# Chunked attention and a gated feed-forward layer on one core: the third block's first product computed plainly, the sums of w_in formed a block later, more output buffers at two boundaries

## The chip, the cores and the metric

The kernel runs on one NeuronCore of a Trainium2 chip. Its engines work side by side and wait for each other through semaphores: TensorE (PE, matmuls; PEld is its weight load), VectorE (DVE), ScalarE (ACT), GpSimd (POOL) and SyncE (SP), which here issues all DMA transfers. The metric is device time in microseconds (us) of one execution; of several runs the median counts.

## The reference, cut to what matters

```python
# q, k, v: 8 batches x 8 heads x 576 tokens x 64, float32;  w_in: 512 x 2048,  w_out: 2048 x 512
# attention inside chunks of 64 tokens
scores = np.matmul(q_c, k_c.transpose(0, 1, 2, 4, 3)) / np.sqrt(64)
scores = scores - np.max(scores, axis=-1, keepdims=True)
attn = np.exp(scores)
attn = attn / (np.sum(attn, axis=-1, keepdims=True) + 1e-09)
x = np.matmul(attn, v_c)            # then heads side by side: 4608 tokens x 512
h = x @ w_in                        # first product, 4608 x 2048
g = h * (1.0 / (1.0 + np.exp(-1.702 * h)))
out = g @ w_out                     # second product, 4608 x 512
```

## The kernel before, in words

The 4608 tokens are 9 blocks of 512 (36 tiles of 128). For each block the first product gives 16 pieces of 128 hidden columns, numbered g = 16n + j for block n; piece g is gated (`g_h`, `g_l`) and goes into the second product, which adds over the 16 pieces into four PSUM banks `po0` to `po3`, one for each tile of the block. At a block's last piece the banks are copied to `ob` buffers (lines 1286 to 1293, ScalarE for tiles 0 and 2, VectorE for 1 and 3) and stored (line 1298). Every matrix is carried as a high and a low word, and a product is three matmuls (low times high, high times high, high times low).

There are three forms of the first product. Blocks 0 and 1 use the plain one (`h_pe`, lines 1245 to 1247): 12 matmuls of 512 columns for each piece. Block 2 (`PLAIN = 2`) uses seven products in place of eight on halves of its own columns (`plan_seven`, lines 693 to 785, matmuls at lines 715 to 717): four phases `ph0` to `ph3` for every two pieces, 7 products of 6 matmuls, each of 256 columns, whose results VectorE and ScalarE add up (`drain_0` to `drain_3`, line 719). Blocks 3 to 8 are taken in pairs, two blocks side by side (`plan_two`, lines 787 to 900, matmuls at 810 to 812): seven products P1 to P7 of 512 columns for every two pieces of both blocks.

The seven products need sums and differences of w_in's parts and of x's parts. `plan_prep` (lines 584 to 649) forms those of w_in while block `PLAIN - 1` runs: GpSimd adds (`whole`, `sums`), ScalarE rounds (`hi`, line 608), VectorE takes the rest (`lo`, line 612), and SP writes the result to the DRAM tensor `seven` (lines 620, 623, 628), from which `plan_seven` (line 702) and `plan_two` (lines 801 and 803) load it. `plan_x` (lines 520 to 582) forms those of x. They stand in the first halves of the tiles `w0` to `w15`, which held w_in until then.

Attention is computed for pairs of tiles (`plan_pair(u)`, u = 4, 6, ... 34). For u from 6 on, 32 or 64 small transfers bring q and k (`load_qk`, lines 953 and 964) into the one buffer `raw`; VectorE transposes them (`tq0`, `tq1`, line 1007), TensorE multiplies (`s`, line 1023), VectorE takes the maximum and subtracts it (`mx`, `m`), ScalarE the exponential, VectorE the sum (`z`), GpSimd divides (line 1053), VectorE transposes again (`et`, line 1072), TensorE multiplies by v (line 1097, together with the next pair's `s`).

The order on each engine is set by the class `Plan`: each step has an engine, a cost, a rank, the events it needs and the buffers it takes and gives, and a list scheduler takes at each moment the ready step of lowest rank. `transfers` in that class is its model of the DMA queue. The order at the start is written out (`ORDER`). Each engine then executes its own list strictly in order. Two buffers `hp` (PSUM) take the first product and the result of attention; a piece's buffer is free when its `g_l` has been formed (line 1272 for plain pieces). The pool `two` holds two `ob` buffers, and the store of one must have landed before it is written again.

Of the kernel before, what the change touches and what calls it, by code (L numbers as in the profile page):

```python
# [9 lines left out]
F32 = mybir.dt.float32  # L10
# [37 lines left out]
class Plan:  # L48
# [8 lines left out]
    ISSUE, LANES, LANDING = 0.48, 8, 2.1  # L57
    TABLE_LOAD = 1.3

    def __init__(self, buffers):  # L60
        self.free = dict(buffers)
        self.steps = []
        self.landed = [0.0] * self.LANES
        self.first = {}


    def add(self, engine, cost, rank, fn, need=(), make=None, take=(), give=(), table=None, port=False):
        self.steps.append((engine, cost, rank, fn, tuple(need), make, tuple(take), tuple(give), table, port or engine == POOL))
# [4 lines left out]
    def transfers(self, now, count, each):  # L73

        for _ in range(count):
            start = max(now, self.landed[-self.LANES])
            now = start + self.ISSUE
            self.landed.append(max(start + self.LANDING, self.landed[-1] + each))
        return now, self.landed[-1]

    def emit(self):
# [18 lines left out]
        while left:  # L100
            for e, heap in ready.items():
                while heap and busy[e] <= now + 1e-9:
# [13 lines left out]
                    _, cost, _, fn, _, make, take, give, tab, port = self.steps[pick]  # L116
# [17 lines left out]
                    post(done, 0, give)  # L134
# [27 lines left out]
def tile_chunk_attention_ffn(  # L162
# [14 lines left out]
    P = 128  # L177
# [14 lines left out]
    RANKS = (-10.5, 9.0, 14.0, 21.0, 26.5, 28.5, 35.0, 39.0, 45.5, 49.5, 61.0, 72.0, 76.5, 85.5, 94.0, 101.5)  # L192
    K_ACT = (1, 2, 3, 4)
    LEAD = 27
    PREP = -3
    SUMS = 3
    ON_POOL = (0,)
    RING_2 = (7, 8, 0, 1, 5, 6)
# [15 lines left out]
    buffers.update({f"half{j}": 0 for j in RING_2})  # L214
# [13 lines left out]
    X_2 = (2, 3, 4)  # L228
    X_SLOT = (9, 10, 11, 12, 6, 2, 3, 7, 15, 5, 13, 14, 4, 8)
# [7 lines left out]

    def run_of(n):

        return (n - PLAIN + 1) // 2  # L240
# [8 lines left out]
    def plan_w(j):  # L249
# [48 lines left out]
        plan.add(DMA, (2, 1.56), rank - 5.5, load, need=need, make=e("raw"), take=[f"w{j}"])  # L298
# [49 lines left out]
    def plan_first(u):  # L348
# [109 lines left out]
        plan.add(DMA, (1, 1.2), u - 103, lambda: load(0), make=ev("q"), take=[slot(0)])  # L458
        plan.add(DMA, (1, 1.2), u - 102.9, lambda: load(1), make=ev("k"))
        plan.add(DMA, (1, 0.9), u - 101.5, load_v, make=ev("v"), take=[slot(1)])  # L460
# [32 lines left out]
    def x_2(i, hl):  # L493

        if i < 4:
            return held["x", i // 2][:, hl, i % 2]
        return wt[X_2[hl]][:, 0, i % 2] if i < 6 else wt[X_2[2]][:, 0, hl]

# [3 lines left out]
    def x_tile(k):  # L502
        held["x", k] = const.tile([P, 2, 2, 512], F32R, tag=f"xe{k}", name=f"xe{k}")

    def staging(u):

        r, i = (0, (u - 8) // 2) if u < 12 else divmod((u - 12) // 2, 4)
        if u < 12:
            return ("sA", "sB")[i]
        return (("sA", "xe2a", "xe2b", "xe3a") if r == 0 else ("sA", "xe3b", "tmp", "tmp"))[i]  # L510
# [9 lines left out]
    def plan_x(r, h, ua, uc, rank):  # L520

        st = {}
        where_t = "xe3b" if r == 1 else "tmp"
        T_ENGINE, T_COST, engine = (POOL, 1.05, nc.gpsimd) if r in ON_POOL else (DVE, 0.69, nc.vector)

        def raw(i, k=1):
# [3 lines left out]
            return d[:, 512 * at : 512 * (at + k)]  # L530
# [6 lines left out]
        def conv(i, k, hl):  # L537
            if r:
                return x_two(i, hl)[:, :, 256 * h : 256 * h + 256]
            if i == 6:  # L540
                return x_2(6, hl)
            t = held["x", i // 2][:, hl] if i < 4 else wt[X_2[hl]][:, 0]
            return t.rearrange("p i f -> p (i f)")

        form = lambda a: a.rearrange("p (c t) -> p c t", c=2) if r else a

        def hi(i, k):
            nc.scalar.activation(conv(i, k, 0), form(raw(i, k)), AF.Copy)

        def lo(i, k):  # L550
            nc.vector.tensor_tensor(conv(i, k, 1), form(raw(i, k)), conv(i, k, 0).bitcast(F32), op=ALU.subtract)

        e = lambda a: f"{a}x_{r}_{h}"
# [6 lines left out]
        for i in (0, 1, 5, 4, 2, 3, 6) if r else (0, 2, 4, 6):  # L560
            k = 1 if r or i == 6 else 2
            need = src[i] + (src[i + 1] if k == 2 else [])
            for hl in range(2):
                j = X_SLOT[2 * i + hl]
                if r == 0:
                    more_need = [f"po_{(X_2[hl] if i < 6 else X_2[2]) // 2}"] if i > 3 else [f"xal_{i // 2}"]
                elif r == 1:
                    g0 = NF * (PLAIN + 1) - 2
                    more_need = [f"po_{j // 2}" if j > 8 else f"ph{(1, 2, 3)[(j in (4, 7, 8)) + (j in (4, 8))]}_{g0}"]
                else:  # L570
                    more_need = [f"{PRODUCT_OF[i]}_{r - 2}_{NF // 2 - 1}"]
# [843 lines left out]
```

## Time and profile before

| | |
|---|---|
| runs | 845.22, 845.10, 842.77 us (median 845.1) |
| profiled execution | 844.18 us, span 842.4 us from first to last instruction |
| TensorE busy | 818.4 us, 97% |
| VectorE, ScalarE, GpSimd busy | 549.1 (65%), 378.4 (45%), 86.7 (10%) |
| mean granted TensorE clock | 0.993 |
| DMA | 128.96 MB, one queue of transfers (q1), 56.5% of 16 engines' span |

The page of the profile gives busy time by engine, the span in 40 slices, the chain of work that ended last, and groups of instructions by line. Where it isn't enough the trace answers by view: waits (who waited for whom), timelines of one engine in a stretch, and busy time with granted clock in a stretch. A clock of 1.00 is 2.4 GHz, 0.50 is 1.2 GHz. Matmuls are pipelined, so their pace is read from the distance of two starts and not from the duration of one.

### The profile page before, as it was taken

The page shows a single profiled execution, that of the slowest core. Times are in us where ns is not written, and L with a number is a line of the kernel's source. Part 1 is how long each engine was busy: PE and PEld are TensorE (multiplying, and loading weights), DVE is VectorE, ACT ScalarE, POOL GpSimd, SP SyncE. Part 2 cuts the span into 40 slices and gives each one's busy share as a digit, 9 for nine tenths or more (in the row PEclk, how much of TensorE's full clock was granted, in tenths as well). Part 3 has the DMA queues.
Part 4 walks back from the last instruction along what each step waited for, and adds up shares of the span by engine and source line. Part 5 has one row for each costly group of instructions (what it writes and reads, how often), then busy time and mean ns, then how long its engine had stood idle before and what let it go on. Part 6 is the DMA issues. An engine that isn't in the chain of part 4 may idle for free.

```text
span 842.4 us, 15212 instructions
## 1 busy us (share of the span) xinstructions
PE 818.4 (97%) x5894; PEld 680.0 (81%) x5894; DVE 549.1 (65%) x781; ACT 378.4 (45%) x557; POOL 86.7 (10%) x78
## 2 busy tenths in 40 slices
PE   7999998999979999999999999999999999999998
PEld 6878886877878888778888888888888888888786
DVE  5769967566867888874776995393778453443422
ACT  5989825345344436342534433342555323223322
POOL 1000163563200000000000100000001000000000
PEclk9999999999989999999999999999999999999999
DMA  9997856775488776575466336466541054444101
GB/s 227 313 309 239 251 130 163 208 202 134 129 244 218 212 209 141 169 175 147 125 179 176 62 79 173 126 152 155 145 128 49 1 165 121 118 122 126 50 1 51
DMA packets 238248, 128.96 MB, mean 153 GB/s; under 512 B 186464, under 2 KB 208992, under 8 KB 238176
## 3 DMA queue, kind: packets, MB, share of 16 engines
q1 hardware_dynamic: 238176, 127.98, 56.5%
q8 instruction: 47, 0.77, 0.4%
q14 instruction: 25, 0.20, 0.1%
HBM read 103.81 MB, written 24.12 MB: 152 GB/s over the span
## 4 chain that ended last, share of the span: by engine, by line
PE 81%; SPq 9%; DMA 4%; DVE 3%; issue 1%; ACT 1%; POOL 0%; DVEq 0%; ACTq 0%; POOLq 0%
PE po L1282 14%; PE po L1283 13%; PE po L1284 13%; PE hp L810 9%; PE hp L811 9%; PE hp L812 9%; SPq L964 3%; SPq L338 2%; PE hp L1245 2%; PE hp L1246 2%; PE hp L1247 2%; DMA w<-seven 2%; PE s L1023 2%; PE x L1097 1%; SPq L258 1%
## 5 line engine op out<-in xcount | busy, mean ns | idle before, releaser
L1282 PE MATMUL po<-w,g_l 128*128 128x512 f32 x576 | 228.1, 396 | 6.7 <-ACT ob L1291 4.8
L1283 PE MATMUL po<-w,g_h 128*128 128x512 f32 x576 | 225.0, 391 | 0.0
L1284 PE MATMUL po<-w,g_h 128*128 128x512 f32 x576 | 224.8, 390 | 0.0
L1282 PEld LDWEIGHTS po<-w,g_l 128*128 128x128 f32 x576 | 108.5, 188 | 32.3 <-ACT ob L1291 5.5
L1284 PEld LDWEIGHTS po<-w,g_h 128*128 128x128 f32 x576 | 108.4, 188 | 23.0
L1283 PEld LDWEIGHTS po<-w,g_h 128*128 128x128 f32 x576 | 108.5, 188 | 21.1
L848 ACT ACTIVATE g<-g 128x512 f32<-128x512 f32 x48 | 30.3, 632 | 143.3 <-DVE g L795 143.1
L1072 DVE STREAM_TRANSPOSE eT<-e 32x512 f32<-32x512 f32 x120 | 84.2, 701 | 5.4 <-POOL e L1053 3.5
L810 PE MATMUL hp<-w,w 128*128 128x512 f32 x224 | 87.4, 390 | 0.2
L811 PE MATMUL hp<-w,w 128*128 128x512 f32 x224 | 87.2, 389 | 0.0
L812 PE MATMUL hp<-w,w 128*128 128x512 f32 x224 | 87.2, 389 | 0.0
L1053 POOL TENSOR_TENSOR e<-e,r 128x1024 f32<-128x1024 f32 x16 | 32.2, 2012 | 502.1 <-DVE r L1050 397.6
L857 DVE TENSOR_TENSOR g_l<-g,g_h 128x512 fp32r<-128x512 f32 x48 | 35.2, 737 | 44.5 <-ACT g_h L853 44.2
L853 ACT ACTIVATE g_h<-g 128x512 fp32r<-128x512 f32 x48 | 30.3, 631 | 73.7 <-PE po L1284 71.4
L1007 DVE STREAM_TRANSPOSE qkT<-raw 128x1024 f32<-128x1024 f32 x30 | 37.2, 1241 | 27.8 <-DMA raw<-in_k_dram 15.7
L1245 PE MATMUL hp<-x_l,w 128*128 128x512 f32 x120 | 47.8, 398 | 5.8 <-DVE g_l L1272 5.8
L810 PEld LDWEIGHTS hp<-w,w 128*128 128x128 f32 x224 | 42.0, 188 | 9.9 <-DVE f L795 0.5
L812 PEld LDWEIGHTS hp<-w,w 128*128 128x128 f32 x224 | 42.0, 188 | 8.8
L811 PEld LDWEIGHTS hp<-w,w 128*128 128x128 f32 x224 | 42.0, 188 | 8.6
L1247 PE MATMUL hp<-x_h,w 128*128 128x512 f32 x120 | 47.4, 395 | 0.0
L1246 PE MATMUL hp<-x_h,w 128*128 128x512 f32 x120 | 47.4, 395 | 0.0
L795 DVE TENSOR_TENSOR d<-hp,d 128x512 f32<-128x512 f32 x48 | 32.9, 684 | 19.0 <-PE hp L812 18.7
(142 smaller groups left out, 1335.5 us busy)
## 6 DMA issues: line engine op xcount, KB each, us to landing
w<-seven SPq DMA_DIRECT2D x120, 256.0 KB, 2.9
pieces<-seven SPq DMA_DIRECT2D x56, 256.0 KB, 2.9
seven<-w SPq DMA_DIRECT2D x24, 512.0 KB, 3.7
w<-seven SPq DMA_DIRECT2D x24, 512.0 KB, 4.6
raw<-in_moe_w_in_dram SPq DMA_DIRECT2D x16, 512.0 KB, 7.5
raw<-in_moe_w_out_dram SPq DMA_DIRECT2D x16, 512.0 KB, 7.8
out_dram<-ob SPq DMA_DIRECT2D x32, 256.0 KB, 2.3
raw<-in_q_dram SPq DMA_DIRECT2D x208, 32.0 KB, 2.4
```

The lines of the kernel that those rows point to most:

```text
L810: nc.tensor.matmul(hp, w[:, 0, c], xl[:, c], start=c == 0, stop=False)
L811: nc.tensor.matmul(hp, w[:, 0, c], xh[:, c], start=False, stop=False)
L812: nc.tensor.matmul(hp, w[:, 1, c], xh[:, c], start=False, stop=c == 1)
L857: nc.vector.tensor_tensor(gl, words(h, late), gh.bitcast(F32), op=ALU.subtract)
L1007: nc.vector.transpose(st["tr"][:, i].rearrange("p n (t j) -> p (n t) j", j=32), st["raw"][:, i].rearrange("p n t j -> p (n t) j"),)
L1072: nc.vector.transpose(st["et"][po : po + 32, :, 32 * a : 32 * a + 32], st["e"][pi : pi + 32, :, 32 * b : 32 * b + 32],)
L1245: nc.tensor.matmul(hp, wh, xl, start=cc == 0, stop=False)
L1246: nc.tensor.matmul(hp, wh, xh, start=False, stop=False)
L1247: nc.tensor.matmul(hp, wl, xh, start=False, stop=cc == NCC - 1)
L1282: nc.tensor.matmul(po, gl[:, c], w[:, 0, :], start=first, stop=False)
L1283: nc.tensor.matmul(po, gh[:, c], w[:, 0, :], start=False, stop=False)
L1284: nc.tensor.matmul(po, gh[:, c], w[:, 1, :], start=False, stop=last)
```

## The change: what it does

`PLAIN` goes from 2 to 3: block 2 gets the plain first product, and `plan_seven` with its loads, drains and buffers is gone, as is the form of `plan_x` that served it. The pairs of blocks are the same three as before (3 and 4, 5 and 6, 7 and 8). Since `plan_prep` runs in block `PLAIN - 1`, the sums of w_in are formed in block 2 and not in block 1. The differences of x for the first pair of blocks (r = 0) are formed by GpSimd where VectorE formed them, and go to other slots (`X_SLOT`).

At the end of blocks 0 and 1 the third and fourth output tile go to buffers of their own (`sA`, `sB`, `xe3b`) in place of the two `ob`; later blocks keep the two.

Of the planner the model of the DMA queue changes (one queue with a bound on the pieces in flight; in both kernels SP issues every transfer, by `nc.sync`), and with it ranks: those of the attention pairs (`RANKS`), of stores (`STORE`, 22 before), of the late gates (`GLATE`, 1.5 before), and single steps moved by `NUDGE`. The written-out `ORDER` of the start is the same.

```diff
+    ISSUE, LANES, LANDING = 0.48, 8, 1.8
+    PIECES = 3072
...
             start = max(now, self.landed[-self.LANES])
+            while True:
+                flight = [(t, n) for t, n in self.flight if t > start]
+                if sum(n for _, n in flight) + pieces <= self.PIECES:
+                    break
+                start = flight[0][0]
             now = start + self.ISSUE
-            self.landed.append(max(start + self.LANDING, self.landed[-1] + each))
+            self.landed.append(max(start + self.LANDING, self.landed[-1]) + each)
+            self.flight = flight + [(self.landed[-1], pieces)]
...
-    RANKS = (-10.5, 9.0, 14.0, 21.0, 26.5, 28.5, 35.0, 39.0, 45.5, 49.5, 61.0, 72.0, 76.5, 85.5, 94.0, 101.5)
+    RANKS = (-2.0, 9.0, 14.0, 20.5, 23.5, 32.5, 33.0, 40.5, 45.0, 55.5, 63.5, 74.5, 74.5, 82.5, 93.5, 100.0)
...
-    ON_POOL = (0,)
+    GLATE = 29.5
+    XLATE = -1.0
+    STORE = 4
...
+    ON_POOL = (0, 3)
...
-    PLAIN = 2
-    TWOS = (NB - PLAIN - 1) // 2
-    START = [NF * (PLAIN + 1) + 30 * s for s in range(TWOS)]
+    PLAIN = 3
+    TWOS = (NB - PLAIN) // 2
+    START = [NF * PLAIN + 30 * s for s in range(TWOS)]
...
-    X_SLOT = (9, 10, 11, 12, 6, 2, 3, 7, 15, 5, 13, 14, 4, 8)
+    X_SLOT = (2, 3, 4, 5, 10, 11, 12, 13, 8, 9, 6, 7, 14, 15)
...
-    def plan_seven(n, p):
...
-        ob_tag = lambda t: ("ob", "ob", "raw", "tr")[t] if n == NB - 1 else "ob"
+        ob_tag = lambda t: {0: ("ob", "ob", "sA", "sB"), 1: ("ob", "ob", "sB", "xe3b"), NB - 1: ("ob", "ob", "raw", "tr")}.get(n, ("ob",) * 4)[t]
...
-            ob = (two if ob_tag(t) == "ob" else const).tile([P, DM], F32, tag=ob_tag(t), name=f"ob_{n}_{t}")
+            if ob_tag(t) in ("sA", "sB", "xe3b"):
+                ob = stage_tile(ob_tag(t), f"ob_{n}_{t}")[:, :DM]
+            else:
+                ob = (two if ob_tag(t) == "ob" else const).tile([P, DM], F32, tag=ob_tag(t), name=f"ob_{n}_{t}")
...
-            if n == PLAIN and j % 2 == 0:
-                plan_seven(n, j // 2)
-            elif n > PLAIN and (n - PLAIN) % 2 and j % 2 == 0:
+            if (n - PLAIN) % 2 == 0 and j % 2 == 0:
                 plan_two((n - PLAIN) // 2, j // 2)
```

How the order moves is shown at three places. The first is VectorE at the end of block 0 and the start of block 1. In the names the first number is the piece, the pair of tiles or the block: `g_l_16` is the low word of piece 16, `qkT_10` the transpose for pair 10, `ob_0_3` tile 3 of block 0; the last number only tells buffers apart. Before:

```order
L1272 TENSOR_TENSOR g_l_15_1348<-hp_15_1287,g_h_15_1347 128x512
L1031 TENSOR_REDUCE m_8_1437<-s_8_1361 128x16
L1111 TENSOR_TENSOR x_l_1_86<-x_6_0_1394,x_h_1_85 128x2x4x64
L1111 TENSOR_TENSOR x_l_1_86<-x_6_1_1395,x_h_1_85 128x2x4x64
L1040 TENSOR_TENSOR e_8_1436<-s_8_1361,m_8_1437 128x1024
L1293 COPY ob_0_1_1482<-po_0_1_442 128x512
L1293 COPY ob_0_3_1495<-po_0_3_533 128x512
L1272 TENSOR_TENSOR g_l_16_1492<-hp_16_1462,g_h_16_1491 128x512
L1007 STREAM_TRANSPOSE qkT_10_1511<-raw_10_1339 128x1024
L1047 TENSOR_REDUCE z_8_1528<-e_8_1436 128x16
```

Now, at the same place:

```order
L919 TENSOR_REDUCE m_8_1436<-s_8_1358 128x16
L999 TENSOR_TENSOR x_l_1_86<-x_6_0_1391,x_h_1_85 128x2x4x64
L999 TENSOR_TENSOR x_l_1_86<-x_6_1_1392,x_h_1_85 128x2x4x64
L1182 COPY ob_0_3_1459<-po_0_3_533 128x512
L1182 COPY ob_0_1_1472<-po_0_1_436 128x512
L928 TENSOR_TENSOR e_8_1435<-s_8_1358,m_8_1436 128x1024
L1158 TENSOR_TENSOR g_l_16_1491<-hp_16_1461,g_h_16_1490 128x512
L935 TENSOR_REDUCE z_8_1522<-e_8_1435 128x16
L936 TENSOR_SCALAR z_8_1522<-z_8_1522 128x16
L938 RECIPROCAL r_8_1525<-z_8_1522 128x16
L895 STREAM_TRANSPOSE qkT_10_1541<-raw_10_1340 128x1024
```

The copies `ob_0_3` and `ob_0_1` now stand ahead of `e_8`, into buffers of their own, and the transpose for pair 10 stands behind the sum `z_8`. The low word of piece 16 still stands behind both copies.

The second place is SP in block 1, from the loads of pair 10 on. `seven<-w` writes sums of w_in, `w<-seven` loads them for block 2, `raw` are the loads of q and k. Before:

```order
L964 DMA raw_10_1339<-in_k_dram 32x8x32 x16
L628 DMA seven_80<-w_0_331 128x1024
L628 DMA seven_80<-w_1_446 128x1024
L702 DMA w_0_331<-seven_80 128x1024
L702 DMA w_1_446<-seven_80 128x512
L628 DMA seven_80<-w_2_530 128x1024
L628 DMA seven_80<-w_3_543 128x1024
L964 DMA raw_12_1662<-in_q_dram 32x8x32 x8
L628 DMA seven_80<-w_4_583 128x1024
L628 DMA seven_80<-w_5_650 128x1024
```

Now:

```order
L852 DMA raw_10_1340<-in_k_dram 32x8x32 x16
L852 DMA raw_12_1619<-in_q_dram 32x8x32 x16
L852 DMA raw_12_1619<-in_k_dram 32x8x32 x12
L356 DMA v_10_1784<-in_v_dram 128x8x64
L852 DMA raw_12_1619<-in_k_dram 32x8x32 x4
L356 DMA v_10_1784<-in_v_dram 128x8x64
L852 DMA raw_14_1836<-in_q_dram 32x8x32 x16
L852 DMA raw_14_1836<-in_k_dram 32x8x32 x16
L356 DMA v_12_2037<-in_v_dram 128x8x64 x2
L841 DMA raw_16_2086<-in_q_dram 32x4x32 x32
```

The sums' writes and the loads for block 2 are gone from between the loads of q and k.

The third place is SP in block 2 of the kernel now, from the loads of pair 18 on (line 619 there is 628 before, line 852 is 964, lines 689 and 691 are 801 and 803):

```order
L852 DMA raw_18_2443<-in_q_dram 32x8x32 x8
L689 DMA pieces_2448<-seven_80 128x2x256 x2
L691 DMA w_0_328<-seven_80 128x512 x2
L691 DMA w_1_440<-seven_80 128x512 x2
L619 DMA seven_80<-w_2_530 128x1024
L852 DMA raw_18_2443<-in_k_dram 32x8x32 x4
L619 DMA seven_80<-w_3_543 128x1024
L852 DMA raw_18_2443<-in_k_dram 32x8x32 x12
L619 DMA seven_80<-w_4_583 128x1024
L619 DMA seven_80<-w_5_644 128x1024
L356 DMA v_16_2756<-in_v_dram 64x8x64 x4
L852 DMA raw_20_2803<-in_q_dram 32x8x32 x12
```

Before, the same loads of pair 18 stood among the loads for `plan_seven`:

```order
L964 DMA raw_18_2715<-in_q_dram 32x8x32 x4
L702 DMA w_0_331<-seven_80 128x1024
L702 DMA w_1_446<-seven_80 128x512
L964 DMA raw_18_2715<-in_q_dram 32x8x32 x8
L338 DMA v_16_2848<-in_v_dram 64x8x64 x2
L964 DMA raw_18_2715<-in_q_dram 32x8x32 x4
L702 DMA w_5_650<-seven_80 128x1024
L964 DMA raw_18_2715<-in_k_dram 32x8x32 x4
L702 DMA w_6_710<-seven_80 128x1024
L338 DMA v_16_2848<-in_v_dram 64x8x64 x2
L702 DMA w_7_754<-seven_80 128x1024
```

The writes of the sums now stand between the loads of q and k of block 2, where the loads of `plan_seven` stood.

## Rows read from the trace of the kernel before

**Rows 1.** The page, part 1: busy us of TensorE (share of the span), instructions.

```profile
PE 818.4 (97%) x5894; PEld 680.0 (81%) x5894; DVE 549.1 (65%) x781; ACT 378.4 (45%) x557; POOL 86.7 (10%) x78
```

**Rows 2.** Waits of TensorE, whole run: waiter, releaser, us, times, longest.

```profile
PE hp L1245 <- DVE g_l L1272: 5.8, 3, 3.3
...
PE po L1282 <- ACT ob L1291: 4.8, 1, 4.8
...
PE po L1282 <- DVE g_l L756: 1.3, 3, 0.5
...
PE hp L715 <- DVE d L719: 0.5, 1, 0.5
...
PE hp L810 <- DVE f L795: 0.5, 1, 0.5
```

**Rows 3.** Timeline, TensorE, first boundary: start us, us, engine, line, operation, [idle before].

```profile
127.00 0.39 PE L1247 MATMUL hp<-x_h,w 128*128 128x512 f32 x1
...
129.72 0.39 PE L1247 MATMUL hp<-x_h,w 128*128 128x512 f32 x1
...
133.45 0.50 PE L1245 MATMUL hp<-x_l,w 128*128 128x512 f32 x1 [3.34 <-DVE g_l L1272]
...
137.90 0.40 PE L1282 MATMUL po<-w,g_l 128*128 128x512 f32 x1
```

**Rows 4.** Timeline, VectorE, first boundary.

```profile
130.97 0.69 DVE L1293 COPY ob<-po 128x512 f32<-128x512 f32 x1 [6.15 <-DMA out_dram<-ob]
...
132.72 0.68 DVE L1272 TENSOR_TENSOR g_l<-hp,g_h 128x512 fp32r<-128x512 f32 x1
```

**Rows 5.** Timeline, transfers issued by SyncE, second block.

```profile
125.02 3.56 SPq L964 DMA_DIRECT2D raw<-in_q_dram  x4
...
128.67 0.87 SPq L1298 DMA_DIRECT2D out_dram<-ob  x2
...
133.38 7.95 SPq L964 DMA_DIRECT2D raw<-in_k_dram  x16
...
206.50 8.86 SPq L953 DMA_DIRECT2D raw<-in_q_dram  x16
```

**Rows 6.** Timeline, TensorE, second boundary.

```profile
235.70 0.28 PE L716 MATMUL hp<-w,w 128*128 128x256 f32 x1
...
235.82 0.28 PE L717 MATMUL hp<-w,w 128*128 128x256 f32 x1
...
240.93 0.79 PE L1282 MATMUL po<-w,g_l 128*128 128x512 f32 x1 [4.83 <-ACT ob L1291]
...
247.32 0.39 PE L1282 MATMUL po<-w,g_l 128*128 128x512 f32 x1
```

**Rows 7.** Timeline, ScalarE, second boundary.

```profile
240.28 0.60 ACT L1291 ACTIVATE ob<-po 128x512 f32<-128x512 f32 x1 [5.95 <-DMA out_dram<-ob]
```

**Rows 8.** Stretch, us, busy PE, PEld, DVE, ACT, POOL, granted clock, DMA share, GB/s.

```profile
134.45:137.87 3.42, 3.42 (x9) 2.63 (x8) 3.35 (x6) 0.12 (x1) 0.73 (x1) 0.50 0.54 106
240.27:247.09 6.82, 6.16 (x23) 5.59 (x24) 4.63 (x11) 4.50 (x5) 1.68 (x1) 0.50 0.74 200
218.72:321.50 102.78, 96.19 (x1037) 85.53 (x1036) 82.74 (x140) 42.99 (x67) 5.72 (x3) 0.97 0.75 201
```

**Rows 9.** Timeline, TensorE, second block.

```profile
182.02 0.50 PE L1245 MATMUL hp<-x_l,w 128*128 128x512 f32 x1 [0.89 <-DVE g_l L1272]
...
202.45 0.50 PE L1245 MATMUL hp<-x_l,w 128*128 128x512 f32 x1 [1.56 <-DVE g_l L1272]
```

**Rows 10.** Timeline, VectorE, second block.

```profile
200.58 1.25 DVE L1007 STREAM_TRANSPOSE qkT<-raw 128x1024 f32<-128x1024 f32 x1 [5.32 <-DMA raw<-in_k_dram]
```

**Rows 11.** Groups of VectorE by line and shape: count, busy us, mean ns, idle before.

```profile
L719 DVE TENSOR_TENSOR d<-hp,d 128x256 f32<-128x256 f32 x40 | 16.7, 418 | 4.0 <-PE hp L717 2.3 <-ACT d L724 0.9
...
L612 DVE TENSOR_TENSOR w<-sums,w 128x512 fp32r<-128x512 f32 x16 | 15.1, 972 | 0.3 <-PE hp L1247 0.3
...
L551 DVE TENSOR_TENSOR w<-xs,w 128x512 fp32r<-128x512 f32 x18 | 12.0, 684 | 0.3 <-ACT w L548 0.3
```

More of the change, by code (lines that the diff above doesn't have):

```diff
@@ L115, in emit @@
                         break
-                    _, cost, _, fn, _, make, take, give, tab, port = self.steps[pick]
+                    _, cost, _, fn, _, make, take, give, tab, port, after = self.steps[pick]
                     if first.get(e):
@@ L133, in emit @@
                     busy[e] = now + cost
-                    post(done, 0, give)
+                    post(done + after, 0, give)
                     if e != DMA:
@@ L297, in plan_w @@
         e = lambda n: f"{n}_{j}"
-        plan.add(DMA, (2, 1.56), rank - 5.5, load, need=need, make=e("raw"), take=[f"w{j}"])
+        plan.add(DMA, (2, 1.5, 384), rank - 5.5, load, need=need, make=e("raw"), take=[f"w{j}"])
         plan.add(ACT, 1.08, rank, scale, need=[e("raw")], make=e("wsc"))
@@ L653, in plan_slots @@
     def plan_slots():
-        for k in range(2):
-            plan.add(None, 0, -1000, lambda k=k: x_tile(k), need=[f"h_{NF * (PLAIN - 1) - 1}"], make=f"xal_{k}")
         def g_tile(k):
@@ L674, in plan_slots @@
         plan.add(
-            None, 0, -1000, piece_tile, need=["l2x_0_0", "l3x_0_0", "t2x_0_0"], make="pieces", take=["sB"],
+            None, 0, -1000, piece_tile, need=["st_1_3"], make="pieces", take=["sB"],
             give=["piece0", "piece1"],
         )
-        last = NF * (PLAIN + 1) - 4
         for i in range(4):
@@ L681, in plan_slots @@
             held["p", 2 + i] = (j, i % 2)
-            plan.add(None, 0, -1000, None, need=[f"ph{2 + j}_{last}"], give=[f"piece{2 + i}"])
+            plan.add(None, 0, -1000, None, need=["po_0"], give=[f"piece{2 + i}"])
     def piece(i):
@@ L878, in plan_two @@
                 else:
-                    need += [f"gal_{p // 2}"] + ([f"{x}_1_{h}" for x in ("l6x", "l3x", "t2x", "l5x", "t4x") for h in range(2)] if p > 3 else [])
+                    need += [f"gal_{p // 2}"] + ([f"{x}_0_{h}" for x in ("l6x", "l3x", "t2x", "l5x", "t4x") for h in range(2)] if p > 3 else [])
             if i == 5:
@@ L903, in o_order @@
     def o_order(n):
[L904 removed]
+        late = n > PLAIN and (n - PLAIN) % 2 == 1
         return [*range(NF - 2, NF), *range(NF - 2)] if late else [*range(NF)]
@@ L1182, in plan_pair @@
         plan.add(
-            ACT, 1.05, rank + 0.6, s_exp, need=[ev("m")] + ([f"gh_{int(rank) + 2}"] if u > NPE and rank < NF * (PLAIN + 1) - 2 else []), make=ev("ex"), table="exp",
+            ACT, 1.05, rank + 0.6, s_exp, need=[ev("m")] + ([f"gh_{int(rank) + 2}"] if u > NPE and rank < NF * PLAIN - 2 else []), make=ev("ex"), table="exp",
         )
```

202 lines of the change are left out of this document (47 added, 155 removed), and 6 rows, old and new, of the table NUDGE.

## The prediction, made before the changed kernel ran

> **What bounds the kernel now.** I read the page first: TensorE is busy 818.4 us, 97% of the span [rows 1], so the time is TensorE's work plus the moments in which it waits. The view of its waits comes next, since nothing else can be shortened without removing work: after the start, three waits for a plain `g_l` (5.8 us together, the longest 3.3), one of 4.8 us for a copy of an output tile, and small ones in block 2, 1.3 and 0.5 us [rows 2]. In blocks 3 to 8 the largest entry is 0.5 us. Then the timelines around the three largest show what released them.
>
> At the first boundary (end of block 0) TensorE's starts lie evenly until 129.72, and the next matmul starts at 133.45 [rows 3]. It wanted an `hp` buffer; the `g_l` that frees one began at 132.72, behind a copy into `ob` that had waited for a store to land [rows 4]. SP had issued the first of these stores at 128.67 [rows 5], late in its queue of q and k loads. At the second boundary the copy on ScalarE at 240.28 waited for a store too [rows 7], and TensorE stood from 235.82 to 240.93 [rows 6]. After each of the two waits the granted clock was 0.50 (1.2 GHz) for 3.42 and 6.82 us [rows 8]: a wait at a boundary is paid a second time.
>
> In block 1 TensorE waited twice more for a `g_l` [rows 9]. For the second one VectorE shows why: the transpose ahead of it waited 5.32 us for loads of k [rows 10]. These loads stand behind writes of w_in's sums in SP's queue, and a write waits there until VectorE has formed the sum.
>
> **The change part by part.** All durations are of the profiled execution: 844.18 us, of which 842.4 are span; the median of the runs, 845.1, is 0.1% above it.
>
> *The product of block 2.* Removed: 8 pairs of pieces x 7 products x 6 matmuls = 336 matmuls of 256 columns. Two starts of that width lie 235.82 - 235.70 = 0.12 us apart [rows 6]: 40.3 us. Added: 16 pieces x 12 = 192 matmuls of 512 columns, at (129.72 - 127.00) / 12 = 0.2267 us [rows 3]: 43.5 us. All of it is on the path, since TensorE is the bound: **+3.2 us**. The attention and second products are the same instructions before and after. With the seven products go their additions on VectorE, 16.7 us for the larger of the two groups [rows 11], in a stretch where VectorE is busy 82.74 of 102.78 us [rows 8], so nothing that it keeps gets less cover.
>
> For the same term the Trainium skill ("TensorE: Matmul & The Clock Gate", Back-to-back issue gap) gives N/2.4 + 2.5 ns at full clock, an estimate of 0.109 and 0.216 us for the two widths, and by it the exchange would cost 192 x 0.216 - 336 x 0.109 = +4.8 us. The trace has 0.12 and 0.2267; the rows decide, and the sum keeps +3.2.
>
> *Four output buffers, first boundary.* The two copies on VectorE need no landed store any more, so `g_l` of piece 16 follows as soon as its gate is done. From 129.72 to 137.90 [rows 3] there are 13 steps of 0.2267 = 2.95 us of work in 8.18 us: 5.2 us are lost, waiting and half clock together. If the wait goes the low clock has no cause: **-5.2 us**. What is late next there: the transpose for pair 10, whose last four q loads now stand behind all four stores, and which stands ahead of `g_l` of piece 17. The first store now comes ahead of the q loads that began at 125.02, and from there on four stores, eight q loads and one of v have to be issued: 13 at 7.95 / 16 = 0.5 us each [rows 5] end at 131.5. If the last lands in time that the transpose runs by 134, `g_l` of piece 17 comes at about 135.5; TensorE, unheld from 129.72, wants its buffer after one piece of first and one of second product, 2 x 12 x 0.2267 = 5.4 us, at 135.2. I put this wait at nothing and keep 1.5 us for it in the range.
>
> *Four output buffers, second boundary.* From 235.82 to 247.32 [rows 6] stand the rest of one step of 0.12, 6 matmuls of 512 and 18 of 256 columns: 0.12 + 1.36 + 2.16 = 3.64 us of work in 11.50 us: **-7.9 us**. There the third and fourth copies go to `sB` and `xe3b`.
>
> *The sums of w_in one block later.* Block 1 loses its two waits, 0.89 and 1.56 us [rows 9]: **-2.5 us**. The waits for `plan_seven`'s `g_l` in block 2, 1.3 and 0.5 us [rows 2], go with that code: **-1.8 us**. But block 2 now holds the mixture that block 1 held: writes of sums between the loads of q and k of pairs 18, 20 and 22, and transposes ahead of `g_l`. No row shows that mixture with a plain block 2. The lower end is no wait at all: SP then has some 130 transfers to issue from the stores of block 1 to those of block 2 (96 of q and k, 16 of sums, 18 others), about 65 us at 0.5 us each [rows 5] against some 100 us of TensorE. The upper end is what the worst single event cost, 7.9 us. I take the rows that show the same mixture, 2.5 us: **+2.5 us**.
>
> *The planner's other moves* (ranks, `NUDGE`, `GLATE`, the bound in `transfers`) change the order of the same instructions. In blocks 3 to 8 there is nearly nothing to win, as the 0.5 us in [rows 2] say. I take 0, between -1 and +2. "All transfers in one queue" changes no queue, since SP issues all of them before as well; 0.
>
> **Sum.** 844.2 + 3.2 - 5.2 - 7.9 - 2.5 - 1.8 + 2.5 = 832.5. The runs' median lies 0.9 above the profiled time and the planner may win a little of the small waits; I predict **832 us**, its own range 828 to 836.
>
> **Rivals.**
>
> *A boundary-sized wait comes back.* From block 2 on the output tiles still share two `ob` buffers, and at the end of block 2 more falls together now than before: the last sums, the last parts of x, the copies, the first gates of the pair. Or the 64 loads of pair 16, which start only when the transpose of pair 14 has freed `raw`, last until block 2 has begun: 16 took 8.86 us [rows 5], 64 at that pace 35.4 us, where a quiet stretch (7.95 for 16) gives 31.8; between them lies whether `g_l` of piece 33, behind the two transposes of that pair, is late. For it: both large waits of now stood at boundaries. Against it: at the end of block 2 no wait over 0.5 us shows now, with two buffers. Price: one more event like the second boundary, 832 + 7.9 = 840.
>
> *Writes of the sums make SP's queue the bound in block 2: slower than before.* Each write waits in SP's queue for VectorE, VectorE's transposes wait for loads behind that write, and `g_l` stands behind the transposes; so one late step feeds the next. If pairs 14 to 22 each met such a wait with the half clock that follows, at the first boundary's price, 5 x 5.2 = 26 us come on top of 830.0, the sum without an allowance: 856. It is slower than before from the fourth such event on (830.0 + 4 x 5.2 = 850.8; three give 845.6). For it: [rows 10] show the first link. Against: the two waits of that kind cost 0.89 and 1.56 us, and the next starts after them came at full pace, and VectorE has lost `plan_seven`'s additions.
>
> *GpSimd's share of the work holds VectorE up at the third boundary.* Both halves of the first x differences are now on GpSimd, eight operations, while VectorE forms the last sums and x parts that TensorE waits for. The same 512-column subtraction took 972 ns on VectorE beside GpSimd's sums (line 612) and 684 ns elsewhere (line 551) [rows 11]: 0.29 us each, and with some ten such operations in one chain near the end of block 2, 3 us; a stretch at half clock as short as the first of [rows 8] loses another 3.42 / 2 = 1.7: 832 + 4.7 = 837.
>
> The Trainium skill ("SBUF — State Buffer", Who interferes with whom) has a VectorE instruction with two SBUF inputs and a GpSimd instruction that reads SBUF exclude each other for a whole instruction. By that rule the trace's 972 ns are a mean over blocked and free operations, and the trace agrees in that the free ones (684 ns) are shorter.
>
> *The change doesn't do what it says:* the stores were not what held the boundaries, and the copies or `g_l` stay late through loads that SP issues late (the first store at 128.67). Then 5.2 and 7.9 stay: 832.5 + 13.1 = 845.6. Against it, [rows 4, 7] name the store itself.
>
> **How the numbers follow.** Forecast 0.60; a boundary-sized wait 0.18; GpSimd 0.07; no gain 0.07; slower 0.08. A difference of 0.3% (2.5 us) is what a measurement can tell here. Faster takes the first three, and a little of the fourth: 0.86; same 0.06; slower 0.08. The range must reach from the sum without any new wait and a small win in the later blocks, 827, to the first rival's 840, which leaves out less than 2 in 10.
>
> **What would show it.** Right: no wait of TensorE for an output copy or for `g_l` at the first two boundaries, and a granted clock of 1.00 through both; 360 + 192 matmuls of the plain product at 0.23 us; block 1 without waits over 0.5 us. The allowance is right if block 2's waits come to 1 to 5 us, for `g_l` behind a transpose that waited for loads. Wrong: a wait over 3 us with clock 0.50 anywhere after 40 us; raw loads behind a write that waits for VectorE, with TensorE idle each time; a distance of two 512-column starts other than 0.227 us.

## The result, and the profile after

The changed kernel takes **833.1 us** (median, 830.2 to 835.4), the kernel before 844.3 in the same session: ratio **0.9855**, 95% interval 0.9825 to 0.9885. Forecast were 832 us and a range of 827 to 840. The number was right, in part by luck. One of the large steps behind it was wrong: the runs below put the second boundary down to the sums that moved, not to the output buffers. And what block 2 gave back was under-priced.

The profiled execution of the changed kernel took 835.4 us, 833.6 of them span. It is the slowest of four, with a mean granted clock of 0.996; the fastest, 830.2 us, had 1.000, so the half clock told below did not come in every run. Its page, part 1 (columns as in [rows 1]), then its waits of TensorE (as in [rows 2]):

```profile
PE 818.4 (98%) x5750; PEld 674.7 (81%) x5750; DVE 525.1 (63%) x717; ACT 368.5 (44%) x543; POOL 93.9 (11%) x82
```

```profile
PE hp L1131 <- DVE g_l L1158: 4.4, 2, 3.6
...
PE hp L1133 <- DVE w L307: 0.5, 1, 0.5
PE hp L698 <- DVE d L683: 0.4, 1, 0.4
```

The wait for an output copy of [rows 2] is gone, and so are its three for a plain `g_l`. Two others have come, a short one at piece 17 and a long one at piece 38. The granted clock, by stretches (columns as in [rows 8]), first across the two boundaries, then behind the long wait (third line):

```profile
122.00:142.00 20.00, 19.14 (x122) 15.49 (x113) 13.53 (x19) 9.83 (x14) 1.91 (x1) 1.00 0.57 128
215.00:240.00 25.00, 25.00 (x230) 20.72 (x229) 14.37 (x17) 12.71 (x20) 7.67 (x8) 1.00 0.59 158
263.27:270.09 6.82, 5.28 (x12) 4.18 (x13) 6.08 (x10) 2.85 (x6) 4.95 (x5) 0.50 0.66 194
```

*First boundary.* VectorE (timeline, columns as in [rows 4]) copies the tiles without waiting for a store; `g_l` of piece 16 follows in time. Piece 17's stands behind the transpose for pair 10, which waited 1.77 us for keys, and TensorE, third fence, idles 0.86 us for it:

```profile
124.92 1.38 DVE L1182 COPY ob<-po 128x512 f32<-128x512 f32 x2 [0.37 <-PE po L1170]
129.58 0.69 DVE L1158 TENSOR_TENSOR g_l<-hp,g_h 128x512 fp32r<-128x512 f32 x1 [2.14 <-ACT g_h L1153]
...
135.43 1.25 DVE L895 STREAM_TRANSPOSE qkT<-raw 128x1024 f32<-128x1024 f32 x1 [1.77 <-DMA raw<-in_k_dram]
136.60 0.65 DVE L1158 TENSOR_TENSOR g_l<-hp,g_h 128x512 fp32r<-128x512 f32 x1
```

```profile
125.65 2.24 SPq L1187 DMA_DIRECT2D out_dram<-ob  x2
```

```profile
137.31 0.50 PE L1131 MATMUL hp<-x_l,w 128*128 128x512 f32 x1 [0.86 <-DVE g_l L1158]
```

The first store (second fence) leaves SP at 125.65, where it was 128.67 in [rows 5].

*The long wait, in block 2, piece 38.* Read it from TensorE back to SP. TensorE waited for `g_l`; VectorE formed it as soon as ScalarE had the gate; ScalarE had stood from 254.0 to 257.47 at a conversion of an x part, which goes into a tile that held sums of w_in and was still being written out:

```profile
264.81 0.80 PE L1131 MATMUL hp<-x_l,w 128*128 128x512 f32 x1 [3.56 <-DVE g_l L1158]
```

```profile
264.07 0.69 DVE L1158 TENSOR_TENSOR g_l<-hp,g_h 128x512 fp32r<-128x512 f32 x1 [0.26 <-ACT g_h L1153]
```

```profile
257.47 0.63 ACT L550 ACTIVATE w<-xs 128x512 fp32r<-128x512 f32 x1 [3.46 <-DMA seven<-w]
258.00 1.14 ACT L550 ACTIVATE w<-g 128x512 fp32r<-128x512 f32 x2
259.16 1.28 ACT L931 ACT_TABLE_LOAD   x1
260.45 1.06 ACT L931 ACTIVATE e<-e 128x1024 f32<-128x1024 f32 x1
261.53 1.28 ACT L1152 ACT_TABLE_LOAD   x1
262.82 0.58 ACT L1152 ACTIVATE hp<-hp 128x512 f32<-128x512 f32 x1
```

```profile
245.00 7.67 SPq L852 DMA_DIRECT2D raw<-in_k_dram  x12
252.77 0.87 SPq L619 DMA_DIRECT2D seven<-w  x2
```

VectorE had formed those sums at 248.05; their two writes were issued only at 252.77, behind 12 loads of keys, and landed 4.6 us later.

**Where the time went.** The table gives the time that TensorE lost between the attention products of successive pairs of tiles, in the profiled executions: the distance of their first matmuls in the timeline, less the work between them (512- and 256-column matmuls at 0.2267 and 0.12 us, attention at 2.03 us a pair). 8-10 holds the first boundary, 14-16 the second. The last four rows are runs told below. A half clock behind a wait is part of what its column lost.

| us lost from pair to pair | 8-10 | 10-12 | 12-14 | 14-16 | 16-18 | 18-20 |
|---|---|---|---|---|---|---|
| before | 5.5 | 1.4 | 2.1 | 8.8 | 1.7 | 1.1 |
| changed | 1.4 | 0.6 | 0.2 | 0.2 | 6.6 | 0.2 |
| before, four buffers | 2.8 | 6.5 | 0.3 | 7.0 | 6.0 | 1.1 |
| before, no sums, two buffers | 4.5 | 0.2 | 0.3 | 1.6 | 2.2 | 1.3 |
| changed, two buffers | 2.5 | 1.0 | 0.2 | 0.3 | 7.1 | 0.2 |
| changed, sums first | 1.1 | 0.8 | 0.2 | 0.2 | 0.7 | 0.2 |

Over these columns the kernel before lost 20.6 us and the changed one 9.2. The difference of 11.4, less 3.2 for the longer product and with 0.6 won elsewhere, is the 8.8 us between the two spans.

### The profile page after: what moved, and what is told of

It reads as the page before. It is cut to its first block, busy times and chain, and to the rows that moved or that the text cites. A ratio compares the mean times of both kernels' runs of the same rounds, so it can differ in the third digit from the quotient of the medians.

```text
span 833.6 us, 14732 instructions
## 1 busy us (share of the span) xinstructions
PE 818.4 (98%) x5750; PEld 674.7 (81%) x5750; DVE 525.1 (63%) x717; ACT 368.5 (44%) x543; POOL 93.9 (11%) x82
## 4 chain that ended last, share of the span: by engine, by line
PE 74%; SPq 14%; DVE 4%; DMA 3%; ACT 2%; issue 2%; DVEq 0%; ACTq 0%
PE po L1168 13%; PE po L1169 13%; PE po L1170 13%; PE hp L698 9%; PE hp L699 9%; PE hp L700 9%; SPq L852 6%; PE hp L1131 2%; PE hp L1133 2%; PE hp L1132 2%; SPq L356 2%; SPq L276 2%; SPq L841 1%; DMA seven<-w 1%; PE s L911 1%
## 5 line engine op out<-in xcount | busy, mean ns | idle before, releaser
L1131 PE MATMUL hp<-x_l,w 128*128 128x512 f32 x184 | 73.3, 398 | 4.6 <-DVE g_l L1158 4.4
L1133 PE MATMUL hp<-x_h,w 128*128 128x512 f32 x184 | 72.7, 395 | 0.5 <-DVE w L307 0.5
L1132 PE MATMUL hp<-x_h,w 128*128 128x512 f32 x184 | 72.6, 394 | 0.0
L1158 DVE TENSOR_TENSOR g_l<-hp,g_h 128x512 fp32r<-128x512 f32 (+1 forms) x50 | 33.1, 663 | 46.8 <-ACT g_h L1153 46.4
L1152 ACT ACTIVATE hp<-hp 128x512 f32<-128x512 f32 (+1 forms) x50 | 28.5, 570 | 55.2 <-PE hp L1133 51.8
L698 PEld LDWEIGHTS hp<-w,w 128*128 128x128 f32 x224 | 42.0, 188 | 9.6 <-DVE d L683 0.8
```

What stands on the lines that cost most here:

```text
L698: nc.tensor.matmul(hp, w[:, 0, c], xl[:, c], start=c == 0, stop=False)
L1131: nc.tensor.matmul(hp, wh, xl, start=cc == 0, stop=False)
L1132: nc.tensor.matmul(hp, wh, xh, start=False, stop=False)
L1133: nc.tensor.matmul(hp, wl, xh, start=False, stop=cc == NCC - 1)
```

## The experiments

All ratios are against the kernel before on the same chip, whose median lay between 847.4 and 848.0 in these sessions; intervals are 95%.

**Were the buffers the cause?** First the changed kernel with its order kept and two buffers (run e1_two_buffers):

```
-            if ob_tag(t) in ("sA", "sB", "xe3b"):
-                ob = stage_tile(ob_tag(t), f"ob_{n}_{t}")[:, :DM]
...
+            tag = "ob" if ob_tag(t) in ("sA", "sB", "xe3b") else ob_tag(t)
...
```

> The changed kernel with its order of instructions untouched, but the third and fourth output tiles of the first two blocks go back into the two buffers of the first pair, so their copies must again wait until the first pair's stores have left. Theory (the stores' landing held the two boundaries): at the first boundary the first pair's two stores are issued on SP at 125.65 (2.24 us for both) and by the kernel before's distance of 5 to 6 us from a store's issue to the copy's start the second pair's copies start near 131 instead of 124.92; VectorE's copy of one column tile then stands ahead of the piece's low part and TensorE waits about 3 to 5 us there with up to 3.4 us of half clock behind it; at the second boundary the first pair's store is issued earlier with SP free, so a wait of 0 to 4 us. Time against the changed kernel +4 to +11 us (837 to 844). Rival (the planner's own earlier stores and the new order had already removed the wait, the buffers were not needed): no new wait over 0.5 us at either boundary and a time within 2 us of the changed kernel's 833.

Measured: 836.5 us, **0.9865** (0.9841 to 0.9890), by its interval not to be told from the changed kernel. The copies wait for stores again, on VectorE 5.30 us at the first boundary, on ScalarE 3.65 us at the second:

```profile
132.56 1.34 DVE L1180 COPY ob<-po 128x512 f32<-128x512 f32 x2 [5.30 <-DMA out_dram<-ob]
```

```profile
227.85 0.60 ACT L1178 ACTIVATE ob<-po 128x512 f32<-128x512 f32 x1 [3.65 <-DMA out_dram<-ob]
```

Only the first costs TensorE anything, 1.98 us in place of the 0.86 above; the second ends before TensorE asks:

```profile
135.69 0.50 PE L1131 MATMUL hp<-x_l,w 128*128 128x512 f32 x1 [1.98 <-DVE g_l L1158]
```

With this order the two extra buffers of a block are worth 1.1 us in the trace (8-10 in the table). The theory's 3 to 5 us and half clock at the first boundary did not come; the rival, which wanted no new wait over 0.5 us, is nearly right. The expectation had misread a row: from the store's issue to the copy's start it is 2.3 us in [rows 4, 5], not 5 to 6; here it was 4.2.

Then the other half alone: the kernel before, its order kept, with four buffers (e3_before_four_buffers):

```
+            own = {(0, 2): "sA", (0, 3): "sB", (1, 2): "xe2b", (1, 3): "xe3b"}.get((n, t))
+            if own:
+                ob = stage_tile(own, f"ob_{n}_{t}")[:, :DM]
...
```

> The kernel before with its order of instructions untouched, but the third and fourth output tiles of the first two blocks have buffers of their own (four for each of these two blocks). Theory (the stores' landing held the boundaries): the copies that waited until 130.97 and 240.28 start as soon as their sums are there; TensorE's waits of 4.78 us at 129.72 and about 4.4 us at 235.82 go or shrink below 1.5 us, the granted clock stays 1.00 there, and the time falls by 8 to 13 us, to 831 to 836. Rival (the next late thing takes the wait's place, because the same transfers are queued on SP and the loads behind them stay late): the waits shrink by half at most, half clock stays in one of the two stretches, and the time falls by 2 to 6 us, to 838 to 842.

Measured: 848.0 us, **1.000** (0.9983 to 1.0017). Both theories fall. No copy waits, but TensorE waits a step further on instead, for a `g_l` behind a transpose that waited for keys: in the table 2.7 and 1.8 us less at the two boundaries, 5.1 and 4.3 us more in the columns 10-12 and 16-18. VectorE and TensorE near the second boundary:

```profile
244.94 1.25 DVE L1007 STREAM_TRANSPOSE qkT<-raw 128x1024 f32<-128x1024 f32 x1 [5.06 <-DMA raw<-in_k_dram]
246.11 1.37 DVE L1072 STREAM_TRANSPOSE eT<-e 32x512 f32<-32x512 f32 x2
247.51 0.69 DVE L756 TENSOR_TENSOR g_l<-d,g_h 128x512 fp32r<-128x512 f32 x1
```

```profile
248.26 0.80 PE L1282 MATMUL po<-w,g_l 128*128 128x512 f32 x1 [3.46 <-DVE g_l L756]
```

SP was late with stores and loads alike (the first store of this boundary left 10.7 us after the first copy's start), and the buffers only chose who waits for it.

**What put SP behind?** The forming and writing of the sums was left out of the kernel before, with two buffers (e8_no_sums_two) and with four (e7_no_sums_four). From here on the later loads of the sums read columns that are still written, so that their number and sizes stay; these kernels leave out work that the result needs.

```
-        plan.add(POOL, 2.4, rank, sums, need=[e("pa")], make=e("psum"), take=["tmp"], give=["tmp"])
+        plan.add(POOL, 2.4, rank, None, need=[e("pa")], make=e("psum"), take=["tmp"], give=["tmp"])
...
-            plan.bulk(1.44, rank, lambda i=i: out_s(i), need=[e(f"plo{i}")], make=e(f"pouts{i}"))
+            plan.bulk(1.44, rank, None, need=[e(f"plo{i}")], make=e(f"pouts{i}"))
...
```

> The kernel before with its two output buffers and, left out, the same forming and writing of w_in's sums. Theory: only block 1's own waits go (0.89 and 1.56 us, and the small ones), and both boundary waits with their half clock stay as they were, since the copies still wait for the stores: ratio 0.994 to 0.998 (-2 to -5 us); the difference between this run and the one with four buffers is then the buffers' worth when the sums are out of the way, 8 to 13 us. Rival (the sums make SP late and so the stores; without them the boundaries cure themselves): the second boundary's wait goes too, ratio 0.983 to 0.990, and the two runs differ by less than 3 us.

> The kernel before with four output buffers at the first two boundaries (as in the run on the kernel before with four buffers, which came out at 1.000 of it) and, left out, the whole forming of w_in's sums: GpSimd's additions, the conversions, and the 16 writes of the sums in block 1; later loads read columns of the same table that are written. All other instructions stand in the same order. Theory (the four buffers remove the boundary waits, but in the kernel before the sums' writes and the work for them in block 1 hold back the loads behind them on SP, and TensorE loses the same time a few pieces later): without the sums the gain stays, no half clock between 125 and 260, ratio 0.981 to 0.988 (-10 to -16 us). Rival (the loads of q and k are late by themselves, paced by the tiles they go into): waits of over 2 us for g_l come back behind transposes that wait for loads, ratio 0.993 to 1.000.

Measured: **0.9844** (0.9815 to 0.9872) with two buffers, **0.9840** (0.9808 to 0.9871) with four. The second boundary's loss falls from 8.8 to 1.6 us without one buffer more: the rival of the run with two buffers was right. SP and ScalarE of that run there:

```profile
193.43 15.04 SPq L953 DMA_DIRECT2D raw<-in_q_dram  x32
...
225.57 1.71 SPq L1298 DMA_DIRECT2D out_dram<-ob  x2
```

```profile
221.72 0.60 ACT L1291 ACTIVATE ob<-po 128x512 f32<-128x512 f32 x1 [5.93 <-PE po L1284]
...
229.34 0.60 ACT L1291 ACTIVATE ob<-po 128x512 f32<-128x512 f32 x1 [0.17 <-DMA out_dram<-ob]
```

The store leaves 3.9 us after the first copy's start. In the kernel before it left 9.9 us after it:

```profile
226.88 0.60 ACT L1291 ACTIVATE ob<-po 128x512 f32<-128x512 f32 x1 [5.93 <-PE po L1284]
```

```profile
236.78 0.85 SPq L1298 DMA_DIRECT2D out_dram<-ob  x2
```

The first boundary lies ahead of the sums and keeps its wait (4.5 us lost); there four buffers do help, 4.5 against 1.5 us lost in the run with four, though the two medians agree within 0.2 us.

So in the kernel before, the sums make the second boundary late, with two buffers as with four. The changed kernel has also dropped the loads for `plan_seven` there and gives its stores another rank; no run takes these apart from the sums.

**What of the sums costs it?** Only the 16 writes left out, with four buffers (e9_unwritten_four; the last pair of lines of the diff above):

> The kernel before with four output buffers at the first two boundaries, the sums formed as before, but left out the 16 writes of them to memory; later loads read columns of the same table that are written. Theory (the writes stand in SP's queue until VectorE has formed a sum, and the loads behind them are what is late): nearly all of the gain of the run without any sums, ratio 0.982 to 0.990. Rival (the work for the sums on GpSimd, ScalarE and VectorE itself delays g_l, for example a transpose that waits for GpSimd's multiplication behind the additions): ratio 0.994 to 1.000, with waits of 2 us or more for g_l in block 1 behind a transpose of e that waits for GpSimd.

Measured: **0.9838** (0.9811 to 0.9866). All of the gain; the work for the sums on GpSimd, ScalarE and VectorE costs nothing that the medians show. Three more runs, with two buffers, take the write apart: its landing cut off from the later loads (e10_no_dependency), an eighth of its size besides (e11_small_writes), and no wait for VectorE (e12_early_writes, with the forming left out and the write kept).

```
-            nc.sync.dma_start(st["w", i][:, : 512 * (b - a)].bitcast(F32), seven[p, :, 512 * a : 512 * b])
+            nc.sync.dma_start(st["w", i][:, : 512 * (b - a)].bitcast(F32), seven[p, :, (512 * a if a == 6 else 0) : (512 * b if a == 6 else 1024)])
...
```

```
-            nc.sync.dma_start(seven[p, :, at : at + 1024], w)
+            nc.sync.dma_start(seven[p, :, at : at + 128], w[:, :128])
```

> The kernel before with its two output buffers, the sums formed and all 16 writes of them made as before; but the later loads of the sums read columns of the same table that were written in block 0, so that no load waits for a sum's write to land (the values are wrong columns, all sizes and places in the order are kept). Without any writes the kernel came out at 0.984. Three theories of what the writes do there. Dependency (a load of the sums stands at the head of SP's queue until the write has landed, and stores and loads behind it are late): most of the gain, ratio 0.984 to 0.990. Queue (a write stands at the head until VectorE has formed the sum, and takes its place of some 0.45 us) and size (8 MB more to move): ratio 0.997 to 1.002.

> As the run without the dependency, and each of the 16 writes of a sum moves 128 columns instead of 1024 (64 KB instead of 512 KB), at the same place in SP's queue and after the same work of VectorE. Size theory (the writes fill the rings and the loads behind them are issued and land more slowly): ratio 0.983 to 0.988, as without the writes, with the 16-fold groups of raw loads at 0.48 to 0.50 us each instead of 0.6 to 0.75. Queue theory (the wait for VectorE and the issue are what counts): ratio 0.995 to 1.001.

> The kernel before with its two output buffers, the forming of the sums left out (GpSimd's additions and the conversions), and the 16 writes made at their places with full size from the tiles of w_in, which are ready since block 0; the later loads read columns written in block 0. So a write never waits for VectorE. Queue theory in its form that the wait for VectorE matters: ratio 0.984 to 0.988. Size theory, and the mere place of 16 x 0.45 us: the loss stays, ratio 0.995 to 1.001.

| run | ratio (95%) | store after first copy's start, 2nd boundary | copy waits for it |
|---|---|---|---|
| before | 1 | 9.9 us | 5.95 us |
| no dependency | 0.9993 (0.9971 to 1.0015) | 10.3 | 6.30 |
| no wait for VectorE | 0.9990 (0.9970 to 1.0009) | 11.4 | 7.49 |
| an eighth of the size | 0.9896 (0.9871 to 0.9922) | 7.3 | 3.04 |
| no sums | 0.9844 (0.9815 to 0.9872) | 3.9 | 0.17 |

By the ratios the size is two thirds of the loss: from 0.9993 it goes to 0.9896 with small writes and to 0.9844 with none. The rest stays with the small writes, and whether it is their places in SP's queue or the wait for VectorE no run shows; that wait alone, taken off the full writes, gave nothing. SP's pace shows the size, in 16 q loads of pair 16 between two pairs of writes, with full writes that never wait (first fence) and with small ones (second); [rows 5] have 8.86 for these 16:

```profile
203.52 8.70 SPq L953 DMA_DIRECT2D raw<-in_q_dram  x16
```

```profile
202.01 7.72 SPq L953 DMA_DIRECT2D raw<-in_q_dram  x16
```

From pair 16's first load to the store SP took 36.4 us with the full writes, 33.3 with the small ones and 32.1 with none.

The Trainium skill ("DMA: Bandwidth & Descriptors", Queues, rings and completion order) has SP own one ring on each of the 16 DMA engines, consumed in ring order. The runs fit this: the same 16 loads took 8.70 us to issue behind 512 KB writes and 7.72 behind 64 KB. How the rings fill no run shows.

**The long wait of the changed kernel.** Two moves on SP alone, in opposite directions, made on the finished order (e2_sums_first, e6_sums_later). Each entry names a step, the step it goes to, and 1 for behind or 0 for ahead of it; `qk_1_3_18` is the last quarter of pair 18's key loads, `pouts1_2` the second of the third part's two writes, `v0_16` the first loads of pair 16's values:

```
+    MOVES = (("qk_1_3_18", "pouts1_2", 1), ("qk_1_2_18", "pouts1_2", 1),)
...
+        for name, to, behind in self.MOVES: step = order.pop(at(name)); order.insert(at(to) + behind, step)
...
```

```
+    MOVES = (("pouts1_2", "v0_16", 1), ("pouts0_2", "v0_16", 1),)
```

> The changed kernel with one move on SP alone: the two steps of 8 loads of pair 18's keys that stand ahead of the third part's two writes of the sums (SP 245.00 to 252.77) go right behind these writes. Theory (ScalarE's conversion at 257.47 waited 3.46 us for the landing of these writes, and with two table loads behind it this made piece 38's g_l late): the writes are issued near 248.1 instead of 252.8, the conversion starts near 254, TensorE's wait of 3.56 us at 260.86 falls below 0.7 us, the half clock from 263.27 to 270.09 goes, and the profiled execution falls by 5 to 6.5 us from its 833.6 span, to 827 to 829; the median falls by 2 to 6 us, to 827 to 831. Rival (ScalarE's string of two conversions, table load, exp and table load is late by itself, or the loads now behind the writes make the transposition late): a wait of 2 us or more stays at piece 38 and the time is within 2 us of 833.

> The changed kernel with the opposite move on SP: the third part's two writes of the sums go behind the next step of loads (pair 16's first half of values, some 2 us of issue) as well. Theory (the landing of these writes sets piece 38): the writes are issued some 2 us later, ScalarE's conversion starts some 2 us later than 257.47, and TensorE's wait at piece 38 grows by 1.5 to 2.2 us, from 3.95 between two matmuls to 5.4 to 6.2, with one stretch of half clock of the same 6.8 us or a shorter one: time +1 to +3 us against 833. Rival (something else on ScalarE or VectorE sets piece 38): no change over 0.5 us in the wait.

Measured with the writes first: 831.0 us, **0.9805** (0.9779 to 0.9830); writes at 249.03, the conversion no longer waits, no half clock anywhere in the run before its end, 5.9 us won between pairs 16 and 18. ScalarE, and the stretch behind piece 38 with its clock of 1.00:

```profile
254.46 1.09 ACT L1008 ACTIVATE g<-x 128x512 f32<-128x512 f32 x2 [4.10 <-PE x L985]
255.44 0.64 ACT L550 ACTIVATE w<-xs 128x512 fp32r<-128x512 f32 x1
```

```profile
255.00:275.00 20.00, 19.90 (x88) 16.12 (x87) 16.81 (x25) 12.56 (x20) 10.08 (x11) 1.00 0.58 141
```

With the writes later, 837.1 us, **0.9869** (0.9844 to 0.9895): against the last operation ahead of it on ScalarE the conversion starts 5.73 us later where it was 4.56, and the distance of TensorE's two matmuls grows by the same 1.17 us, from 3.95 to 5.12. That is less than expected, since the write, now behind two loads of values and not directly behind the keys, landed in 3.2 us instead of 4.6:

```profile
255.37 1.09 ACT L1008 ACTIVATE g<-x 128x512 f32<-128x512 f32 x2 [4.10 <-PE x L985]
261.10 0.63 ACT L550 ACTIVATE w<-xs 128x512 fp32r<-128x512 f32 x1 [4.64 <-DMA seven<-w]
```

By the ratios its time lies 1.2 us above the changed kernel's, inside both intervals; the place is shown by the trace.

**A version that beats both.** Six moves (e5_three_moves), then nine more (e13_nine_more: `pout1_4` and both `pout` of 5, 6 and 7 behind `qk_1_3_14`, `v0_10` and `v1_10` behind `qk_1_3_12`), by the same list:

```
+    MOVES = (("qk_1_3_18", "pouts1_2", 1), ("qk_1_2_18", "pouts1_2", 1), ("w_10", "tq0_6", 0), ("wshift_13", "gl_9", 1), ("st_0_3", "qk_0_3_10", 1), ("st_0_1", "qk_0_3_10", 1),)
```

> The changed kernel with six steps moved: (a) on SP, the 8 loads of pair 18's keys behind the third part's writes of the sums, as in the run that did this alone (ratio 0.9805); (b) on SP, the stores of tiles 1 and 3 of block 0 behind the last four q loads of pair 10; (c) on VectorE, the low part of w_10 ahead of the transpose for pair 6, and the shift of w_13 behind g_l of piece 9. Theory (each of these is a wait of its own, none covers for another): the wait of about 1.0 us at piece 17 goes, and the waits at 83 and 89 us (1.0 + 0.5 between two starts, 0.8 + 0.2 beyond the distance) go: another 1.5 to 2.5 us, 828 to 830 where the run with (a) alone had 831.0, ratio 0.977 to 0.979. Rival (TensorE's next late thing takes what they give, as it did with four buffers alone in the kernel before): within 0.5 us of the run with (a) alone.

> The run of the changed kernel with six steps moved (0.9789), and nine more moved on SP: seven of the writes of w_in's own columns, which stand among the loads of pair 8 (95 to 118 us), go behind pair 14's last loads, where SP is idle from 182 to 188 us; the two loads of pair 10's values go behind pair 12's last keys. Theory (the transposes at 119.0 and 165.2, which waited 4.0 and 3.3 us for their loads, are late by SP's issue alone): the waits of TensorE at 118.9 (1.1 us) and 165.6 (1.1 us) shrink below 0.5 us each, ratio 0.976 to 0.978, 1 to 2.2 us below 830.5. Rival (the loads are held by the tiles they go into, which VectorE's earlier transposes free): both waits stay, same time within 0.5 us.

Measured: 830.5 us, **0.9789** (0.9765 to 0.9814), and 828.6 us, **0.9798** (0.9772 to 0.9824). The six moves beat both kernels; they cannot be told from the one move (0.9805). The waits at 83, 88 and 136 us went, and part of them came back at 118.9 and 165.6 behind transposes that waited 4.0 and 3.3 us for keys:

```profile
119.01 1.25 DVE L895 STREAM_TRANSPOSE qkT<-raw 128x1024 f32<-128x1024 f32 x1 [4.01 <-DMA raw<-in_k_dram]
...
165.24 1.25 DVE L895 STREAM_TRANSPOSE qkT<-raw 128x1024 f32<-128x1024 f32 x1 [3.26 <-DMA raw<-in_k_dram]
```

The nine more miss the 0.976 to 0.978 expected of them. They end the wait at 118.9 and shorten the one at 165.6 to 0.5 us, and then TensorE is early enough at piece 38 to wait 2.29 us for a `g_l`, by way of a transpose that waits for the keys put behind the writes (VectorE, then TensorE). With 3.4 us of half clock behind it TensorE lost 4.7 us between pairs 16 and 18, where with six moves it lost 0.7:

```profile
256.65 1.25 DVE L895 STREAM_TRANSPOSE qkT<-raw 128x1024 f32<-128x1024 f32 x1 [2.97 <-DMA raw<-in_k_dram]
...
260.56 1.28 DVE L1158 TENSOR_TENSOR g_l<-hp,g_h 128x512 fp32r<-128x512 f32 x2
```

```profile
261.29 0.50 PE L1131 MATMUL hp<-x_l,w 128*128 128x512 f32 x1 [2.29 <-DVE g_l L1158]
```

## Why the prediction was right in its number and wrong in a cause

*The product of block 2, +3.2: held.* The distance of 512-column starts stayed 0.227 us.

*First boundary, -5.2: 4.1 came, by two causes.* The wait for the store went. The wait named as late next (piece 17's `g_l` at 135.5 against 135.2) did come, `g_l` at 136.60, and cost 1.0 us where I had put nothing. Of the 4.1 the buffers gave 1.1 in the new order; the rest is left to the earlier store on SP and the new order on VectorE, which no run tried alone.

*Second boundary, -7.9: 8.6 came, but not from the buffers.* This is the step that failed. [Rows 7] name a store, and I took its landing for the cause. The store had left late, 9.9 us after the first copy's start, because SP was late, and SP was late through the sums' writes of block 1: without the sums 1.6 of the 8.8 us stay, with four buffers alone 7.0. "The sums one block later" should have carried the 7.9, the buffers nothing. Had only the buffers been changed, my steps would have said -13.1, and the run says 0.

*Sums one block later, block 1, -2.5: 2.7 came* (columns 10-12 and 12-14 of the table).

*Block 2, -1.8 + 2.5: +4.0 came* (columns 16-18 and 18-20). The allowance was the mis-sized term: in the profiled execution one event of 6.3 us, not 2.5. Its mechanism was the one I had reversed: not loads behind a write, but a write behind loads, and a conversion that needs the written tile. My upper end, 7.9, covered it.

*The planner's other moves, 0: 1.2 us lost* at 83 and 88 us, where the transpose for pair 6 now stands ahead of w_10's low part, and 1.2 won in 20-24 and small sums elsewhere.

*The rivals.* A boundary-sized wait did come back, at neither of the two places named, with the long stretch at 0.50 that I had listed as a sign of being wrong. SP's queue as the bound was real in block 1 of the kernel before; in block 2 of the changed one it showed once, not five times. GpSimd held nobody up at the third boundary: 0.4 us lost between pairs 20 and 22. "The stores were not what held the boundaries" I gave 0.07: right for the second, only that the change cured it by another of its parts. So the right sum was luck in this point: errors of 7.9 in two terms cancelled because both edits were made together.

## What to carry to other kernels

When a wait names a transfer that landed late, ask first when its engine issued it, and what stood ahead in that queue: a queue that is behind makes everything behind it late, and taking away one waiter only shows the next. While the queue was behind, four buffers for two gave nothing (1.000). Leave out the bulk traffic once to see who pays for it. An in-place buffer that is being written out is a dependency of whatever reuses it, so put its write ahead of bulk loads, and then look at who waits for those loads: in the last run TensorE did.

## What the hardware showed that was not expected

- In the kernel before, sixteen writes of 512 KB each cost 13 us of 847. It gave nothing to free the later loads from their landing, or the writes from their wait for VectorE; with 64 KB each at the same places, 8.8 us came back.
- A wait's price at half clock differs, and the length of the wait alone does not decide it. Behind a distance of 3.95 us between two matmuls (changed kernel) the granted clock was 0.50 for 6.82 us, behind 2.67 us (nine more moves) and 2.21 us (an eighth of the size, second boundary) for 3.41 us each. Behind 2.71 us (before, four buffers, first boundary) and 2.37 us (changed, two buffers) it stayed at 1.00.
